# New instruction lists, and new transfer costs in the planner, for a chunk-selecting attention followed by an ELU feed-forward layer

## The chip, the cores and the metric

The kernel runs on one core of a Trainium2 chip. The metric is the device time of one execution in microseconds. It is given as the median of several executions; a profile is taken of one execution, and has a time of its own.

## The reference

Four batches, eight heads, 768 positions, head size 64. Keys stand in 24 chunks of 32. For each query an upper bound of its score with every chunk is computed from the chunk's least and greatest key, and the six best chunks at or before the query's own are kept. Attention runs over the keys of these chunks (and only over earlier positions). The eight heads' results, side by side, go through a layer of 512 to 2048 and back with an ELU between.

```python
k_min, k_max = np.min(k_chunks, axis=3), np.max(k_chunks, axis=3)
ub = np.sum(np.maximum(q[..., None, :] * k_min[:, :, None], q[..., None, :] * k_max[:, :, None]), axis=-1)
ub = np.where(causal, ub, -1e9)
top_chunks = np.argsort(ub, axis=-1)[..., -6:]
scores = scale * np.matmul(q, k.transpose(0, 1, 3, 2))
scores = np.where(sel & (pos[:, None] >= pos[None, :]), scores, -1e9)
attn = softmax(scores)            # written out with max, exp, sum + 1e-9
x = (attn @ v).transpose(0, 2, 1, 3).reshape(3072, 512)
h = x @ w_in
out = np.where(h > 0, h, np.exp(np.minimum(h, 0)) - 1) @ w_out
```

Inputs and output are float32; the products run in bfloat16.

## The kernel before

Heads are handled in pairs (16 pairs, four for each batch), each in two halves of 384 queries. The steps of a pair, with the lines that the profile shows:

- Loads. The four pairs of batch 0 come in halves through staging tiles `gT` (`first_prep`: k and q at L663, v at L668). All later pairs come whole into tiles `f` (`pair_prep`: k and q at L592 in four transfer starts each, 128-byte packets; v at L634 in two starts). SP issues nearly all of them; four q loads of the start are issued by ACT; POOL issues the eight weight transfers (`weights`, L560 and L564).
- Preparation. Batch 0: TensorE transposes (L685), ACT copies out of PSUM (L695, L717, L721), DVE chunk minima and maxima (L704, L711). Later pairs: DVE block transposes (L604, L622) and reductions (L608), ACT L625. POOL casts to bfloat16 (L737, and L728 or L638 for v).
- Selection, for two pairs at once (`quad_sel`): TensorE bounds (L771), DVE transpose, maxima, comparison and transpose back (L787, L799, L804, L810), POOL puts the selection into extra rows of the query tile (L821).
- Attention (`pair_attend`): TensorE scores (L863), ACT exp (L890), POOL causal cut (L909), TensorE values (L922), DVE normalisation (L935, L938), TensorE transpose (L947), ACT copy (L950).
- Feed-forward for half a batch (`mlp`): TensorE up (L972), ACT exp and, in some steps, relu (L982, L987), DVE ELU (L990, L1000, L1005, L1011, L1016), TensorE down (L1032, in four parts for each of three row tiles), ACT copy to one of three `osb` buffers (L1041), SP store (L1046).

The program is straight-line code, and each engine executes its own list in order. The order is not left to a scheduler: every operation gets a number as it is added to a plan, and `QUEUE` holds, for each of the five engines, the numbers in the order in which they are to be emitted. `Plan.order` walks the five lists with a small model of the machine (durations, PSUM and SBUF buffers as numbered slots, the TensorE clock, and the transfers in `served`); from this clock come the order in which the lists are merged into one program and the buffer that each operation gets. The order on each engine is that of the list, whatever the model says. An operation waits, on the chip, for the data that it reads and for the buffer that it takes.

Operations that are spoken of below, by number:

- 13, 31, 47, 65: SP's loads of k, first half, of pairs 0, 1, 2, 3; 163, 181, 197, 215: the second halves; 165, 183, 199, 217: q, second halves; 17, 51, 167, 201: v loads of three starts each. On PE, 19, 35, 53, 69 transpose the first halves of k.
- 331, 333, 335, 337: POOL's transfers of `w_in`; 339 to 345: of `w_out`.
- 415, 421, 427 and 497, 503, 509: ACT's copies of the first six output tiles to `osb`; 416, 422, 428, 498, 504, 510: SP's stores of them.
- 915, 964, 966 (L592, four starts each), 961 (L634, two starts): loads of later pairs.
- 1097 with 1098, and 1091 with 1092: scores on PE (L863) with their exp on ACT (L890).

A list is walked like this, and an operation starts no earlier than its inputs, its buffers and its list allow:

```python
turn = {e: [ops[n] for n in QUEUE[e]] for e in QUEUE}
...
o = turn[e][0]
r = max(t, o.ready)
```

Of the kernel before, what the change touches and what calls it, by code (L numbers as in the profile page):

```python
# [85 lines left out]
    ],  # L86
    "ACT": [
# [20 lines left out]
    ],  # L108
# [5 lines left out]
    ],  # L114
# [43 lines left out]
class Plan:  # L158
# [71 lines left out]
    SHARE = {128: 1.0, 256: 0.35, 512: 0.3, 768: 0.3, 1024: 0.3, 2048: 0.5}  # L230
    HEAVY = 0.088
    RAMP = 240.0
    PAUSE = ((0.0, 2.28), (17.2, 17.8), (21.6, 22.4), (30.5, 31.3))
    LANDED = 0.75

    def served(self, rings, t, until):

        while True:
# [5 lines left out]
            for a, b in self.PAUSE:  # L244
                if a <= t < b:
                    heads = []
# [867 lines left out]
```

## Time and profile before

| | us |
|---|---|
| median of three runs | 273.88 |
| lowest, highest | 272.23, 274.41 |
| the profiled execution | 273.46 |
| its span, first to last instruction | 271.8 |
| TensorE busy in it | 258.6 |
| DVE, ACT, POOL busy | 206.8, 200.0, 118.3 |

The granted TensorE clock was 0.998 of full speed. The profile page gives one execution: busy time of each engine, 40 slices of the span, DMA queues, the chain of work that ended last, the costliest groups of instructions with the idle time before them and what ended it, and DMA issues. Further views of the same trace give busy time by stretch, waits by pair of lines, the chain in order of time, and timelines of an engine. PE is TensorE's products, PEld its weight loads, SPq SyncE's queue.

### The profile page before, as it was taken

The numbers are of one execution on the slowest core, as the hardware profiler recorded it, in microseconds if no ns is written. First come the engines' busy times: TensorE is split into PE (matmuls) and PEld (weight loads), VectorE is DVE, ScalarE is ACT, GpSimd is POOL, SyncE is SP. The second block draws the span as 40 slices with busy tenths as digits, with TensorE's granted clock in tenths as the row PEclk, the third lists the DMA queues.
The fourth block names the chain that finished last, engine by engine and source line by source line (L and its number), as shares of the span: only waits on it lengthen the run. The fifth ranks groups of instructions, "written<-read, shape, count | busy, mean of one in ns | idle before, by whom it ended". The sixth has DMA issues, their size and how long they took to land.

```text
span 271.8 us, 6603 instructions
## 1 busy us (share of the span) xinstructions
PE 258.6 (95%) x2456; PEld 160.0 (59%) x2456; DVE 206.8 (76%) x532; ACT 200.0 (74%) x375; POOL 118.3 (44%) x209
## 2 busy tenths in 40 slices
PE   3898899999999899999999999999999999999995
PEld 3787566655565455655565556665666655555544
DVE  5698979899999979889998867786666875137530
ACT  3899999846996589989899478977898744243512
POOL 3577783155876696870874055544330000000000
PEclk9999999999999999999999999999999999999999
DMA  7997999999999995999931010000210101110113
GB/s 218 266 211 124 205 216 214 164 176 151 148 203 130 192 169 115 139 156 201 240 103 41 1 58 22 0 2 3 76 41 1 41 2 39 39 41 0 65 53 116
DMA packets 112624, 29.79 MB, mean 110 GB/s; under 512 B 101200, under 2 KB 109648, under 8 KB 112592
## 3 DMA queue, kind: packets, MB, share of 16 engines
q1 hardware_dynamic: 107280, 24.39, 48.5%
q0 software_dynamic: 4224, 4.19, 9.3%
q10 hardware_dynamic: 1088, 0.79, 0.9%
q8 instruction: 19, 0.31, 0.5%
q14 instruction: 13, 0.11, 0.1%
HBM read 27.26 MB, written 6.29 MB: 123 GB/s over the span
## 4 chain that ended last, share of the span: by engine, by line
PE 78%; ACT 7%; DVE 6%; DMA 6%; issue 1%; SPq 1%; POOL 0%; DVEq 0%; ACTq 0%; POOLq 0%
PE psH L972 20%; PE psM L1032 20%; PE psS L863 10%; PE psS L972 8%; PE psMT L1032 8%; PE psO L922 6%; ACT pt L890 3%; DMA w_in_sb<-in_moe_w_in_dram 3%; PE psS L771 2%; ACT lhs L695 2%; PE psT L947 2%; DMA out_dram<-osb 1%; PE psMT L685 1%; DMA gT<-in_k_dram 1%; PE psH L685 1%
## 5 line engine op out<-in xcount | busy, mean ns | idle before, releaser
L890 ACT ACTIVATE pt<-psS 128x768 bf16<-128x768 f32 (+1 forms) x120 | 89.8, 781 | 11.3 <-PE psS L863 6.7
L972 PE MATMUL psH<-xT,w_in_sb 128*128 128x384 bf16 x384 | 73.7, 326 | 0.5 <-DMA w_in_sb<-in_moe_w_in_dram 0.4
L1032 PE MATMUL psM<-w_out_sb,gT 128*128 128x512 bf16 x288 | 72.1, 379 | 0.0
L972 PEld LDWEIGHTS <-w_in_sb 128*128 128x128 bf16 x512 | 47.7, 97 | 33.1 <-issue 1.3
L863 PE MATMUL psS<-rhs,lhs 88*128 88x384 bf16 (+4 forms) x304 | 54.6, 283 | 2.8 <-ACT pt L890 2.8
L1032 PEld LDWEIGHTS <-gT 128*128 128x128 bf16 x400 | 37.3, 97 | 33.0 <-DVE gT L1016 0.5
L982 ACT ACTIVATE f<-psH 128x384 f32<-128x384 f32 x96 | 47.0, 506 | 7.0 <-PE psH L972 6.1
L909 POOL TENSOR_SCALAR_AFFINE_SELECT pt<-pt 128x512 bf16<-128x512 bf16 (+1 forms) x48 | 24.7, 522 | 61.6 <-ACT pt L890 58.1
L1011 DVE SCALAR_TENSOR_TENSOR t<-f,psH 128x384 bf16<-128x384 f32 x56 | 30.1, 547 | 12.9 <-ACT f L982 12.4
L863 PEld LDWEIGHTS <-lhs 88*128 88x128 bf16 x304 | 27.4, 98 | 17.8 <-issue 3.0
L737 POOL CAST rhs<-f 64x768 bf16<-64x768 f32 (+1 forms) x40 | 27.7, 698 | 20.4 <-DVE f L622 8.6
L821 POOL COPY rhs<-selt 24x576 bf16<-24x576 bf16 (+2 forms) x40 | 22.7, 566 | 24.2 <-DVE selt L810 22.5
L922 PEld LDWEIGHTS <-pt 128*128 128x128 bf16 x672 | 28.3, 98 | 7.4 <-issue 1.0
L1016 DVE SCALAR_TENSOR_TENSOR gT<-psH,t 128x384 bf16<-128x384 f32 x56 | 30.5, 551 | 1.1
L922 PE MATMUL psO<-vext,pt 128*128 128x65 bf16 x672 | 31.1, 194 | 0.1
L950 ACT ACTIVATE xT<-psT 128x384 bf16<-128x384 bf16 x32 | 15.6, 497 | 11.9 <-PE psT L947 11.9
L972 PE MATMUL psS<-xT,w_in_sb 128*128 128x384 bf16 x128 | 22.9, 326 | 0.0
L982 ACT ACTIVATE f<-psS 128x768 f32<-128x768 f32 x16 | 13.0, 811 | 13.5 <-PE psS L972 13.5
L990 DVE SCALAR_TENSOR_TENSOR gT<-f,psH 128x384 bf16<-128x384 f32 x40 | 21.3, 541 | 2.0 <-ACT psH L987 1.3
L1032 PE MATMUL psMT<-w_out_sb,gT 128*128 128x512 bf16 (+1 forms) x112 | 22.6, 349 | 0.0
L737 POOL CAST lhs<-f 64x768 bf16<-64x768 f32 x24 | 19.7, 823 | 6.4 <-DVE f L604 5.5
L987 ACT ACTIVATE psH<-psH 128x384 f32<-128x384 f32 x40 | 20.2, 512 | 0.0
(55 smaller groups left out, 278.9 us busy)
## 6 DMA issues: line engine op xcount, KB each, us to landing
out_dram<-osb SPq DMA_DIRECT2D x23, 256.0 KB, 2.2
f<-in_k_dram SPq DMA_DIRECT2D x48, 96.0 KB, 3.9
f<-in_q_dram SPq DMA_DIRECT2D x48, 96.0 KB, 3.8
f<-in_v_dram SPq DMA_DIRECT2D x24, 192.0 KB, 3.9
w_in_sb<-in_moe_w_in_dram POOLq DMA_DIRECT2D x4, 512.0 KB, 9.2
w_out_sb<-in_moe_w_out_dram POOLq DMA_DIRECT2D x4, 512.0 KB, 14.7
gT<-in_k_dram SPq DMA_DIRECT2D x8, 192.0 KB, 4.3
gT<-in_v_dram SPq DMA_DIRECT2D x12, 128.0 KB, 4.2
```

Of the source, the lines that this page charges most:

```text
L737: nc.gpsimd.tensor_copy(out=o, in_=i)
L821: eng.tensor_copy(out=dst.rearrange("c h (i two x) -> c h i two x", two=2, x=32)[:, :, :, odd, :], in_=tiles[st][r0:r0 + NCH, c0:c0 + n].r ...
L863: nc.tensor.matmul(p_s[:, hd, pc:pc + w], lhsT=tiles[pt_["kb"]][0:64 + NCH, hd, 128 * kb:128 * kb + 128], rhs=tiles[pt_["qb"]][0:64 + NCH, ...
L890: lambda bs=bs, pt=pt, wtot=wtot, lo=lo, at=at: nc.scalar.activation(out=tiles[pt][:, :, lo:lo + wtot], in_=tiles[bs[0]][:, :, at:at + wto ...
L909: nc.gpsimd.affine_select(out=a, in_=a, compare_op=AOT.is_ge, fill=0.0, base=0, pattern=pat, channel_multiplier=-1)
L922: nc.tensor.matmul(po[:, hd, qi, :], lhsT=tiles[pt][:, hd, off:off + 128], rhs=tiles[pt_["vx"]][:, 6 * hd + kb, :], start=(kb == 0), stop= ...
L972: nc.tensor.matmul(ph, lhsT=w_in_sb[:, kk, f0:f0 + 128], rhs=tiles[XT[4 * b + kk]][:, c0:c0 + HALF], start=(kk == 0), stop=(kk == NKK - 1))
L982: lambda e=e, view=view: nc.scalar.activation(out=halves(e)[:, 0:step], in_=view(), func=AF.Exp),
L990: lambda e=e, view=view, fc=fc, gt=gt: nc.vector.scalar_tensor_tensor(out=tiles[gt][:, fc:fc + step, :], in0=halves(e)[:, 0:step], scalar= ...
L1011: lambda e=e, t=t, view=view: nc.vector.scalar_tensor_tensor(out=tiles[t][:, 0:step], in0=halves(e)[:, 0:step], scalar=1.0, in1=view(), op ...
L1016: lambda t=t, view=view, fc=fc, gt=gt: nc.vector.scalar_tensor_tensor(out=tiles[gt][:, fc:fc + step, :], in0=view(), scalar=0.0, in1=tiles ...
L1032: nc.tensor.matmul(pm, lhsT=tiles[gt][:, fc, 128 * tt:128 * tt + 128], rhs=w_out_sb[:, fc, x0:x1], start=(fc == 0), stop=(fc == NFC - 1))
```

## The change

All five lists are replaced. Each holds the same numbers as before in another order: of PE's 574 places 485 hold another operation, of DVE's 370, 252, of ACT's 378, 285, of POOL's 196, 164, of SP's 77, 53. No operation moves to another engine, and none is added or dropped. The planner's model of transfers changes too: more pauses, the start of a weight transfer as a delay, another share where two queues carry packets of different size, another start delay of ACT's loads, and a later landing of weight parts.

SP's list up to the store of operation 422, before and after (starts are counted from the code: one for each load of batch 0's k and q, three for its v, four for L592, two for L634, one for a store):

```diff
-        13, 163, 31, 47, 17, 65, 165, 217, 183, 51, 181, 197, 201, 215, 199, 511, 167, 513, 528, 530, 545, 525,
-        559, 562, 547, 564, 913, 542, 915, 944, 961, 576, 930, 932, 947, 964, 428, 927, 949, 1317, 498, 978,
-        504, 966, 1315, 1334, 1329, 1349, 1366, 1346, 1332, 422, 1368, 1363, 510, 1351, 416, 818, 1380, 824,
+        13, 31, 65, 47, 17, 51, 163, 183, 165, 197, 181, 167, 215, 199, 201, 217, 511, 513, 528, 530, 545, 559,
+        525, 562, 547, 564, 542, 913, 576, 947, 944, 932, 930, 428, 915, 964, 961, 949, 498, 927, 978, 966,
+        1317, 504, 1315, 422, 1332, 1334, 1349, 1366, 1346, 416, 510, 1368, 1351, 1329, 1380, 818, 1363, 824,
```

The start of PE's list, ACT's around copy 497, POOL's around transfer 331, and PE's and ACT's around 1097 and 1098:

```diff
 PE
-        19, 25, 35, 41, 59, 53, 69, 75, 169, 81, 106, 175, 90, 191, 185, 122, 203, 131, 93, 209, 219, 225, 147,
+        19, 35, 25, 41, 53, 69, 59, 75, 81, 169, 191, 106, 175, 185, 122, 203, 90, 93, 219, 209, 131, 231, 225,
 ACT
-        ... 482, 625, 483, 486, 490, 696, 692, 677, 497, 715, 694,
+        ... 482, 483, 486, 490, 692, 696, 715, 497, 677, 712, 694,
 POOL
-        ... 128, 212, 213, 229, 331, 228, 238, 237, 333, 335, 239, 240, 337, 180, 339, 341, 287, 343, 288,
+        ... 212, 127, 130, 128, 129, 331, 228, 229, 213, 237, 238, 333, 335, 239, 240, 180, 519, 288, 287, 337,
 PE
-        ... 827, 875, 1008, 1064, 828, 1097, 879, 1091, 996, 1000, 999, 998, 997, 1001, 863, 843, 871, 1383,
-        1095, 855, 895, 901, 887, 1081, 1082, 1084, 1083, 1085, 1086, 896, 1113, 891, 902, 1131, 903, 1100,
+        ... 827, 883, 828, 1135, 1091, 863, 871, 843, 1383, 855, 887, 891, 895, 901, 902, 903, 896,
+        996, 998, 999, 1000, 997, 1001, 897, 1097, 1113, 1004, 1064, 904, 1081, 1082, 1084, 1085, 1083, 1086,
 ACT
-        ... 1092, 864, 844, 845, 1098, 872, 865, 873, 856, 1096, 888, 1114, 892, 1377, 905, 1005, 1132,
+        ... 864, 844, 845, 872, 873, 829, 856, 888, 1377, 892, 1092, 1005, 1114, 1098, 1065, 899, 1101,
```

The planner:

```diff
-    ALONE = {128: 0.0138, 256: 0.0188, 512: 0.036, 768: 0.0368, 1024: 0.055, 2048: 0.085}
+    ALONE = {128: 0.0138, 256: 0.0188, 512: 0.036, 768: 0.0376, 1024: 0.055, 2048: 0.085}
...
-    PAUSE = ((0.0, 2.28), (17.2, 17.8), (21.6, 22.4), (30.5, 31.3))
+    PAUSE = ((0.0, 2.28), (17.2, 18.0), (21.8, 22.6), (30.5, 31.3), (53.0, 54.0), (61.0, 62.0), (67.0, 68.2), (80.6, 81.6), (85.4, 86.2), (98.0, 99.0), (108.0, 109.0), (117.0, 118.0))
...
             if heavy and heavy[0][4]:
-                heavy[0][1] += self.RAMP
+                heavy[0][0] = t + self.RAMP * self.HEAVY / 16
                 heavy[0][4] = 0
+                continue
...
+            if not heavy and len(heads) == 2:
+                (e0, h0), (e1, h1) = heads
+                c0, c1 = self.ALONE[h0[2]], self.ALONE[h1[2]]
+                if max(c0, c1) > 1.5 * min(c0, c1):
+                    rate[e0] = 16 / c0 * (0.75 if c0 < c1 else 0.25)
+                    rate[e1] = 16 / c1 * (0.75 if c1 < c0 else 0.25)
...
-        add("DMA", 0.0, -20.0, lambda: None, reads=[("asked", i)], writes=[name], lat=plan.LANDED)
+        add("DMA", 0.0, -20.0, lambda: None, reads=[("asked", i)], writes=[name], lat=plan.LANDED + (0.8 if i else 0.3))
...
-            move=(0 if eng == "SP" else 1, 1.08 if eng == "SP" else 1.3, 0.533, starts, packets, size), **kw)
+            move=(0 if eng == "SP" else 1, 1.08 if eng == "SP" else 1.75, 0.533, starts, packets, size), **kw)
```

The changed file is seven lines longer from `served` on, so L663 before is L670 after, and so on for every line number above.

156 rows, old and new, of the table QUEUE are left out of this document.

## The prediction

> **What bounds the kernel now.** I read the page first, then busy time by stage, then the chain, the waits and the timelines of the places where TensorE stands.
>
> ```profile
> span 271.8 us, 6603 instructions
> ...
> PE 258.6 (95%) x2456; PEld 160.0 (59%) x2456; DVE 206.8 (76%) x532; ACT 200.0 (74%) x375; POOL 118.3 (44%) x209
> ```
>
> The next rows are stretches of the span: length, then busy time of PE, weight load, DVE, ACT and POOL, the granted clock, the DMA share (it counts overlapping packets, so it can pass 1) and GB/s.
>
> ```profile
> 4.20:14.00 9.80, 8.82 (x90) 7.54 (x91) 6.18 (x19) 7.45 (x17) 4.26 (x9) 1.00 1.15 286
> 14.00:35.00 21.00, 18.87 (x315) 15.43 (x313) 19.57 (x84) 20.11 (x46) 15.81 (x32) 1.00 1.11 179
> 35.00:57.00 22.00, 21.51 (x241) 14.40 (x238) 19.36 (x39) 18.80 (x36) 10.01 (x17) 1.00 1.24 195
> 57.00:98.00 41.00, 39.00 (x350) 21.68 (x348) 40.31 (x104) 30.38 (x55) 28.64 (x45) 1.00 1.14 164
> 98.00:210.00 112.00, 112.00 (x1090) 68.00 (x1089) 89.97 (x235) 96.58 (x184) 56.49 (x92) 1.00 0.39 79
> 210.00:258.00 48.00, 48.00 (x322) 26.87 (x320) 26.91 (x43) 22.57 (x36) 0.64 (x1) 1.00 0.08 31
> 258.00:271.80 13.80, 10.44 (x65) 6.06 (x62) 2.56 (x4) 2.77 (x5) 0.00 (x0) 0.96 0.24 88
> ```
>
> Four regimes follow. From 14 to 35 us ACT is the full engine (20.11 of 21). From 57 to 98 DVE is (40.31 of 41), with PE close behind. From 98 to 258 PE never stands: 160 of 160. The last 13.8 us are the final products and their stores. A list that orders the same instructions can win only where PE, or the engine that PE follows, stands: before 98 us. After that it can only lose.
>
> PE's records overlap, so "busy" needs a second reading, the pitch in the chain (start, length, what):
>
> ```profile
> 95.93 1.73 PE psM L1032 x8
> ...
> 115.27 0.65 PE psH L972 x4
> ...
> 119.17 0.86 PE psM L1032 x4
> ```
>
> Four products of L1032 advance the chain by 0.86 us and four of L972 by 0.65, and from 95.93 us on the chain is made almost wholly of such pieces of PE. I take the full PE stretches as truly full.
>
> The Trainium skill (Perfetto Trace Analysis, section Identifying the Most-Contended Engine) holds that matmul busy time does not measure the headroom of TensorE and that the share of weight loads does. By that rule 59% would leave 111 us of room on PE, and a new order could win much more than I allow. The pitch in the chain does not agree: the room is in the waits alone.
>
> **The change, part by part.** No instruction is added, removed or resized; durations stay. The cost constants steer only the planner's clock, which merges the fixed lists and picks buffers, so they issue nothing: 0 us. What acts are the places in the five lists.
>
> (1) *The store that holds ACT at 93 us* (88 to 95 us).
>
> ```profile
> 84.84 4.94 SPq L592 DMA_DIRECT2D f<-in_k_dram  x8
> 89.82 0.61 SPq L1046 DMA_DIRECT2D out_dram<-osb  x1
> ...
> 89.82 3.55 DMA out_dram<-osb
> ...
> 90.84 0.81 ACT L890 ACTIVATE pt<-psS 128x768 bf16<-128x768 f32 x1 [0.17 <-PE psS L863]
> 93.39 0.60 ACT L1041 ACTIVATE osb<-psM 128x512 f32<-128x512 f32 x1 [1.74 <-DMA out_dram<-osb]
> ...
> 94.74 0.49 PE L863 MATMUL psS<-rhs,lhs 88*128 88x384 bf16 x2 [1.36 <-ACT pt L890]
> 95.44 0.48 PE L863 MATMUL psS<-rhs,lhs 88*128 88x384 bf16 x2 [0.22 <-ACT pt L890]
> ```
>
> Two of the three `osb` buffers hold outputs whose stores (416, 422) stand far down SP's list, so one buffer rotates. Its store, 428, issues at 89.82 behind loads and lands 3.55 us later; ACT's next copy (497) waits 1.74 us for it, the exps behind the copy wait too, and PE stands 1.36 + 0.22 = 1.58 us. In the new SP list 428 stands ahead of 915, 964 and 961: 4 + 4 + 2 = 10 starts fewer. Eight starts take 4.94 us, so ten take 6.2: issue near 83.6, landing near 87.2. ACT reaches the copy at 90.84 + 0.81 = 91.65 (on ACT's list 497 only trades places with one exp), so 4.5 us to spare, and the wait goes. How much of 1.58 stays won? DVE is next to be late:
>
> ```profile
> 91.00:98.00 7.00, 5.42 (x38) 2.81 (x36) 6.64 (x10) 4.76 (x8) 4.78 (x9) 1.00 1.35 189
> ```
>
> DVE stands only 7 - 6.64 = 0.36 us here. If DVE binds, 0.36 is all; if its next results are early enough, 1.58. DVE's order puts loads' transposes between PE's needs and has slack from 98 on (89.97 of 112), so I take the middle: -1.0 (bounds -1.58 to -0.36).
>
> (2) *The first loads* (0 to 14 us).
>
> ```profile
> 0.81 1.97 SPq L663 DMA_DIRECT2D gT<-in_k_dram  x4
> ...
> 6.04 0.51 SPq L663 DMA_DIRECT2D gT<-in_k_dram  x1
> ...
> 12.22 1.57 SPq L668 DMA_DIRECT2D gT<-in_v_dram  x3
> ...
> 14.71 0.51 SPq L663 DMA_DIRECT2D gT<-in_q_dram  x1
> ...
> 7.04 0.49 ACT L717 ACTIVATE f<-psMT 128x384 f32<-128x384 f32 x1 [0.80 <-PE psMT L685]
> ...
> 12.01 0.48 ACT L695 ACTIVATE lhs<-psH 64x384 bf16<-64x384 f32 x1 [0.49 <-PE psH L685]
> ...
> 11.13 0.85 PE L685 MATMUL psH<-ident_f,gT 128*128 128x128 f32 x6 [0.87 <-ACT qa L721]
> ...
> gT<-in_k_dram SPq DMA_DIRECT2D x8, 192.0 KB, 4.3
> ```
>
> The old list sends a second-half k (163) as SP's second load and the fourth pair's first-half k (65) as its eighth, at 6.04; the transposes of that one start at 11.13, 5.1 us later. The new list sends 13, 31, 65, 47: 65 issues near 1.8 with the first group. The ACT waits at 7.04 and 12.01, 0.80 + 0.49 = 1.29 us, are what this can win, since ACT is full right after. Against it: the last k/q load (217) now stands one v load (three starts, 1.57 us by the row) behind the place where the last one was, so near 16.3, and a load takes 4.3 us. What comes in earlier at first comes in later at the end. Bounds: -1.29, and +1.57 if the late load goes wholly through to ACT. The transposes that need 217 stand some 5 us after its issue, 0.7 more than a load takes, so I stay nearer the gain: -0.5.
>
> The Trainium skill (DMA: Bandwidth & Descriptors, section Issuing engines are not separate DMA queues) states that transfers of all issuing engines share the same 16 DMA engines and interleave. The stage's DMA share of 1.15 agrees that they are full; by that rule reordering moves lateness about, this term is 0, and the sum would be 0.5 us higher.
>
> (3) *The weights* (24 to 36 us).
>
> ```profile
> PEld L972 <- DMA w_in_sb<-in_moe_w_in_dram: 0.5, 1, 0.5
> ...
> 23.33 1.52 POOL L737 CAST rhs<-f 64x384 bf16<-64x384 f32 x3 [0.97 <-ACT f L717]
> 24.79 0.92 POOL L560 DMA_DIRECT2D w_in_sb<-in_moe_w_in_dram  x1
> ```
>
> The first weight transfer (331) stood behind three casts and now stands behind one of them: two casts fewer, 1.52 / 3 = 0.51 each, 1.0 us earlier. PE's one wait for weights is 0.5. I take -0.3 (0 to -0.5). The later w_out parts move back on POOL, behind transfers that are still queued: 0.
>
> (4) *SP's own wait*.
>
> ```profile
> 99.55 1.06 SPq L634 DMA_DIRECT2D f<-in_v_dram  x2
> 104.48 0.36 SPq L1046 DMA_DIRECT2D out_dram<-osb  x1
> ```
>
> Store 504 held SP from 100.61 to 104.48; now load 966 goes first. Behind it are loads for POOL and DVE; PE does not stand there (112 of 112), so 0.
>
> (5) *Everything else*: nearly every operation changes place by a few positions. In the full PE stretch this cannot win; a result that comes one step late costs. I take +0.3; the bounds are 0 and the fourth rival's 3.5.
>
> **Sum**: -1.0 - 0.5 - 0.3 + 0.3 = -1.5 us. The profiled execution took 273.46 us (271.8 span, 1.66 around it); it would become 271.96. The median of the runs before is 273.88, 0.42 above it, so the forecast is 273.88 - 1.5 = 272.4 us; its own range is 271.0 to 273.6.
>
> **The rivals.**
> *All waits go* (B): 1.58 + 1.29 + 0.5 = 3.4, nothing lost after 98 us: 270.5. For it: each wait has a visible cause that the lists move the right way. Against: ACT and DVE are full behind them, so a shift must pass through both.
> *The new lists do not help* (C): the store's wait goes and DVE (40.31 of 41) takes its place; the early loads even out: 273.9.
> *Slower* (D): an exp that ACT reaches before its scores, at 147 us.
>
> ```profile
> 143.30 0.49 PE L863 MATMUL psS<-rhs,lhs 88*128 88x384 bf16 x2
> ...
> 147.27 0.80 ACT L890 ACTIVATE pt<-psS 128x768 bf16<-128x768 f32 x1
> ...
> 147.00:154.00 7.00, 7.00 (x75) 3.75 (x75) 6.07 (x14) 4.61 (x10) 0.62 (x2) 1.00 0.01 4
> 154.00:161.00 7.00, 7.00 (x55) 3.92 (x54) 5.67 (x25) 4.04 (x9) 2.66 (x4) 1.00 0.10 37
> ```
>
> Scores 1097 move behind seven L972 groups (0.65 each in the chain), six L1032 groups (0.86) and some small ones, about 11 us; their exp 1098 moves back only some nine ACT operations of about 0.5, 4.4 us. Its lead was 147.27 - 143.79 = 3.5, so ACT would stand 11 - 4.4 - 3.5, about 3 to 3.5 us, with its list blocked. If a product group's exp (L982) is needed meanwhile, PE stops as long: 272.4 + 3.5 = 275.9, and up to 278 if the neighbour (1091, 1092) does the same. Against it: ACT has 2.39 + 2.96 = 5.35 us free in these 14 us, and in the new list the L982 exps of this stage all stand ahead of 1098. It decides only if ACT's wait outlasts that cover.
>
> **How the numbers follow.** Forecast 0.48, B 0.15, C 0.12, D 0.25. About 1%, 2.7 us, is what a measurement of this kernel can tell from no change: under 271.1 is faster, over 276.6 slower. Faster: B 0.15 and the low end of the forecast 0.08, 0.23. Slower: a little over half of D, 0.14. Within 1%: 0.63. The range 270.4 to 276.6 leaves out about half of B and the top of D.
>
> **What would show it.** Right: ACT's copy at about 91 us without a DMA wait and store 428 issued before 85; the fourth first-half transpose of k starting before 11; weights issued near 23.5 and no PE wait on them; PE still full from 98 to 258. Wrong: DVE over 6.9 of 7 from 91 to 98 with PE waiting on it (C); ACT waiting over 3 us for L863 near 150 with PE short of full there (D); new PE waits on k or q loads between 15 and 25 us.

## The result, and the profile after

| | before | after |
|---|---|---|
| median of five runs, us | 273.68 | 271.17 |
| lowest, highest | 272.23, 274.41 | 270.49, 271.98 |
| the profiled execution, its span | 273.46, 271.8 | 271.23, 269.5 |

The new lists are faster: ratio 0.9913 [0.9887, 0.9939], 2.5 us. In a second set of runs the same kernel gave 0.9948 [0.9917, 0.9979], about 1.4 us. The ratios, here and below, are estimated from single runs of the fast state and are not the quotients of the medians beside them, from which they differ by up to 0.003.

The head of the page, then the stretches of the span as in the prediction (length, then PE, weight load, DVE, ACT, POOL, granted clock, DMA share, GB/s), all of the kernel after:

```profile
span 269.5 us, 6606 instructions
...
PE 257.1 (95%) x2431; PEld 159.9 (59%) x2456; DVE 206.2 (77%) x532; ACT 199.8 (74%) x375; POOL 118.7 (44%) x209
```

```profile
4.20:14.00 9.80, 9.02 (x92) 7.76 (x93) 8.76 (x28) 7.77 (x18) 3.63 (x8) 1.00 1.19 285
14.00:35.00 21.00, 18.64 (x301) 14.77 (x298) 18.25 (x78) 19.85 (x46) 15.88 (x32) 1.00 1.06 177
35.00:57.00 22.00, 21.78 (x247) 14.97 (x250) 19.63 (x39) 19.57 (x37) 11.36 (x18) 1.00 1.23 193
57.00:98.00 41.00, 40.41 (x377) 23.18 (x380) 40.62 (x106) 32.39 (x57) 29.69 (x46) 1.00 1.09 169
98.00:210.00 112.00, 111.35 (x1060) 67.67 (x1069) 88.71 (x237) 96.13 (x185) 55.03 (x90) 1.00 0.40 81
210.00:258.00 48.00, 47.70 (x311) 26.43 (x316) 27.39 (x42) 20.43 (x33) 0.64 (x1) 1.00 0.09 34
```

PE gains 1.4 us of work between 57 and 98 us. Behind 98 us it seems 0.95 us short of full, but the trace lacks 25 of its 2456 products (x2431), so the busy time is not the place to read a loss.

**A ledger from three rows.** ACT's copies of the output tiles are the same work in both kernels. Three of them, operation 415, operation 497 and the last one, cut the span in four. First their rows before (that of 497, at 93.39, stands in the prediction), then after, in ACT's timeline (start, length, and in brackets the idle time ahead of it and who ended it):

```profile
60.69 0.60 ACT L1041 ACTIVATE osb<-psM 128x512 f32<-128x512 f32 x1 [1.61 <-PE psM L1032]
...
268.53 0.38 ACT L1041 ACTIVATE osb<-psMT 128x256 f32<-128x256 f32 x1 [0.97 <-PE psMT L1032]
```

```profile
60.25 0.60 ACT L1048 ACTIVATE osb<-psM 128x512 f32<-128x512 f32 x1 [1.61 <-PE psM L1039]
...
91.00 0.59 ACT L1048 ACTIVATE osb<-psM 128x512 f32<-128x512 f32 x1
...
266.29 0.38 ACT L1048 ACTIVATE osb<-psMT 128x256 f32<-128x256 f32 x1 [1.36 <-PE psMT L1039]
```

| us | to 415 | 415 to 497 | 497 to last copy | last copy to end |
|---|---|---|---|---|
| before | 60.69 | 32.70 | 175.14 | 3.27 |
| after | 60.25 | 30.75 | 175.29 | 3.21 |
| difference | -0.44 | -1.95 | +0.15 | -0.06 |

The sum is -2.30, the difference of the spans. Most of it lies between 415 and 497, where the wait of 1.74 us for a store is gone from the row of 497. The store now issues here, in SP's timeline:

```profile
83.75 0.48 SPq L1053 DMA_DIRECT2D out_dram<-osb  x1
```

### The profile page after: what moved, and what is told of

Read it like the earlier page. It is cut to its first block, busy times and chain, and to the rows that moved or that the text cites. A ratio compares the mean times of both kernels' runs of the same rounds, so it can differ in the third digit from the quotient of the medians.

```text
span 269.5 us, 6606 instructions
## 1 busy us (share of the span) xinstructions
PE 257.1 (95%) x2431; PEld 159.9 (59%) x2456; DVE 206.2 (77%) x532; ACT 199.8 (74%) x375; POOL 118.7 (44%) x209
## 4 chain that ended last, share of the span: by engine, by line
PE 82%; DVE 7%; DMA 4%; ACT 3%; issue 2%; POOL 1%; DVEq 0%; POOLq 0%; ACTq 0%
PE psH L979 22%; PE psM L1039 20%; PE psS L870 10%; PE psS L979 8%; PE psMT L1039 8%; PE psO L929 6%; DMA w_in_sb<-in_moe_w_in_dram 3%; PE psS L778 3%; PE psT L954 2%; PE psH L692 1%; ACT lhs L702 1%; DMA gT<-in_k_dram 1%; DVE f L611 1%; DVE f L629 1%; DVE kx L615 1%
## 5 line engine op out<-in xcount | busy, mean ns | idle before, releaser
L897 ACT ACTIVATE pt<-psS 128x768 bf16<-128x768 f32 (+2 forms) x120 | 89.4, 780 | 13.6 <-PE psS L870 6.8
L979 PE MATMUL psH<-xT,w_in_sb 128*128 128x384 bf16 x384 | 74.7, 326 | 0.7 <-DMA w_in_sb<-in_moe_w_in_dram 0.5
L1039 PE MATMUL psM<-w_out_sb,gT 128*128 128x512 bf16 x266 | 68.5, 379 | 1.2
L870 PE MATMUL psS<-rhs,lhs 88*128 88x384 bf16 (+4 forms) x304 | 53.7, 283 | 0.2
L929 PEld LDWEIGHTS <-pt 128*128 128x128 bf16 x672 | 26.9, 98 | 5.8 <-issue 0.3
L929 PE MATMUL psO<-vext,pt 128*128 128x65 bf16 x672 | 29.1, 193 | 0.1
```

The lines of the kernel that those rows point to most:

```text
L870: nc.tensor.matmul(p_s[:, hd, pc:pc + w], lhsT=tiles[pt_["kb"]][0:64 + NCH, hd, 128 * kb:128 * kb + 128], rhs=tiles[pt_["qb"]][0:64 + NCH, ...
L897: lambda bs=bs, pt=pt, wtot=wtot, lo=lo, at=at: nc.scalar.activation(out=tiles[pt][:, :, lo:lo + wtot], in_=tiles[bs[0]][:, :, at:at + wto ...
L929: nc.tensor.matmul(po[:, hd, qi, :], lhsT=tiles[pt][:, hd, off:off + 128], rhs=tiles[pt_["vx"]][:, 6 * hd + kb, :], start=(kb == 0), stop= ...
L979: nc.tensor.matmul(ph, lhsT=w_in_sb[:, kk, f0:f0 + 128], rhs=tiles[XT[4 * b + kk]][:, c0:c0 + HALF], start=(kk == 0), stop=(kk == NKK - 1))
L1039: nc.tensor.matmul(pm, lhsT=tiles[gt][:, fc, 128 * tt:128 * tt + 128], rhs=w_out_sb[:, fc, x0:x1], start=(fc == 0), stop=(fc == NFC - 1))
```

## The experiments

The theory after the result: the store 428 alone carries most of the gain; it was under-priced; the early terms carry little. The rivals: the new middle part wins by its whole order, not by the store; or the early loads win and the store is chance. Every run stands beside runs of the kernel before on its own chip; ratios are to those.

**Only the store, and thirds of the new lists.** The first takes the lists of before and moves one number on SP:

```diff
-    576, 930, 932, 947, 964, 428, 927,
+    576, 930, 428, 932, 947, 964, 927,
```

> The lists of before; on SP's list alone the store 428 stands ahead of 932 instead of behind 964 (932, 947, 964: twelve load starts fewer ahead of it). Theory 1 (the wait of ACT's copy for this store is the main gain): the copy no longer waits, 1.2 to 1.8 us faster than before, 0.994 to 0.996. Rival 2 (DVE binds there, and it is the new lists of DVE, PE and ACT between 57 and 105 us that win): ACT's wait goes but DVE takes its place, 0 to 0.4 us.

The next three take the new order on all five engines in one part of the span and the old one in the others; all three carry the planner of after. The cuts are where both orders have emitted the same set of operations: about 57 and 105 us.

```diff
 QUEUE, each engine: old | old | old
+mid:                old | new | old
+first57:            new | old | old
+late:               old | old | new
```

> The lists of before up to about 57 us and from about 105 us on, the new lists between. Theory 1: the store's wait is in this part, 1.5 to 2.0 us faster than before (0.993 to 0.995). Rival 2: about the same, 1.8 us, and more than the run with the store alone by over 1 us. Rival 3 (the gain is spread over all stages): 0.8 us.

> The new lists up to about 57 us, the lists of before from there. Theory 1: the first loads and the weights come out even or win little, 0.2 to 0.6 us faster than before (0.998 to 0.999). Rival 3 (spread): 0.8 us. With the store's wait still in, the gain may also be swallowed at 93 us: then 0.

> The lists of before up to about 105 us, the new lists after it. Theory 1: PE is full there in both, so 0.0 us, within 0.2. Rival 3: 0.5 to 0.8 us faster. The forecast's own term for small losses there: 0.3 us slower.

| | median, us | before, us | ratio |
|---|---|---|---|
| store | 272.08 | 273.02 | 0.9949 [0.9927, 0.9972] |
| mid | 271.66 | 273.02 | 0.9944 [0.9921, 0.9967] |
| first57 | 273.63 | 273.02 | 0.9994 [0.9964, 1.0024] |
| late | 273.54 | 273.02 | 1.0005 [0.9979, 1.0032] |

The one moved store, and the middle part that holds it, gain 0.5% each; the other two parts gain nothing that can be measured. `late` carries the planner's new costs, and `store` the old ones, so the gain does not come from the planner. Copies 415, 497 and last in `store`:

```profile
60.96 0.60 ACT L1037 ACTIVATE osb<-psM 128x512 f32<-128x512 f32 x1 [1.61 <-PE psM L1028]
...
91.82 0.59 ACT L1037 ACTIVATE osb<-psM 128x512 f32<-128x512 f32 x1
...
266.96 0.38 ACT L1037 ACTIVATE osb<-psMT 128x256 f32<-128x256 f32 x1 [0.98 <-PE psMT L1028]
```

From 415 to 497 it takes 30.86, against 32.70 before and 30.75 with all new lists: of the 1.95 us of that stretch the single store carries 1.84 in these profiles. Behind 497 `store` takes 175.14, to the hundredth what before takes: nothing of the gain is given back. Copies 415 and 497 in `mid`, 30.75 apart, then all three in `late`:

```profile
60.78 0.60 ACT L1044 ACTIVATE osb<-psM 128x512 f32<-128x512 f32 x1 [1.61 <-PE psM L1035]
...
91.53 0.59 ACT L1044 ACTIVATE osb<-psM 128x512 f32<-128x512 f32 x1
```

```profile
60.73 0.60 ACT L1044 ACTIVATE osb<-psM 128x512 f32<-128x512 f32 x1 [1.61 <-PE psM L1035]
...
93.27 0.60 ACT L1044 ACTIVATE osb<-psM 128x512 f32<-128x512 f32 x1 [1.56 <-DMA out_dram<-osb]
...
269.05 0.38 ACT L1044 ACTIVATE osb<-psMT 128x256 f32<-128x256 f32 x1 [1.36 <-PE psMT L1035]
```

`late` keeps the wait (32.54), and takes 175.78 behind 497, 0.64 more than before.

`first57` asks where early gains go. Copies 415 and 497 in its profile, and in the chain the flight of the store that 497 waits for:

```profile
59.38 0.60 ACT L1044 ACTIVATE osb<-psM 128x512 f32<-128x512 f32 x1 [1.61 <-PE psM L1035]
...
91.27 0.60 ACT L1044 ACTIVATE osb<-psM 128x512 f32<-128x512 f32 x1 [0.32 <-DMA out_dram<-osb]
```

```profile
88.74 2.50 DMA out_dram<-osb
```

It comes to 415 1.31 us earlier than before does. With the store in its old place SP issues it at 88.74, at the end of an unbroken row of loads, as before does at 89.82. In this profile the store thus came 1.08 us earlier too and flew 2.50 us instead of 3.55, and the early gain was kept: this execution (271.33) was the fastest of twelve with a median of 273.63. That in the other executions a later issue or a usual flight eats the early gain is argued; the next run has a profile of such a case.

**The store alone put back, and the kernel after once more.** In the new lists:

```diff
-    930, 428, 915, 964, 961, 949,
+    930, 915, 964, 961, 428, 949,
```

> The changed kernel with the store 428 alone put back behind 915, 964 and 961 on SP's list (ten load starts). Theory 1 (ACT's wait for this store is the main term): the wait of about 1.5 us comes back and most of the gain goes, 1.2 to 1.8 us slower than the changed kernel, 0.995 to 0.998 of before. Rival 2 (DVE binds, the store does not matter in the new lists): as fast as the changed kernel, within 0.4 us.

> The changed kernel once more, on the chip of the next three, to compare with them: 0.990 to 0.994 of before.

The lists of after with the store put back took 275.43 us beside 273.45 of before, 1.0054 [1.002, 1.0088]; after again took 272.29, 0.9948 [0.9917, 0.9979]. One number in one list is thus worth about 3 us here (3.1 by the medians, 2.9 by the ratios), and without it the new lists are slower than the old; expected was that they would stay a little faster. Copies 415 and 497 of the kernel with the store put back, and the flight in its chain:

```profile
59.61 0.60 ACT L1044 ACTIVATE osb<-psM 128x512 f32<-128x512 f32 x1 [1.61 <-PE psM L1035]
...
93.05 0.60 ACT L1044 ACTIVATE osb<-psM 128x512 f32<-128x512 f32 x1 [2.56 <-DMA out_dram<-osb]
```

```profile
89.21 3.81 DMA out_dram<-osb
```

At 415 it is 1.08 us ahead of before; at 497 it is 0.34 ahead. ACT waits 2.56 instead of 1.74: what came early waits longer for a store that SP issues behind its loads (at 89.21) and that flies 3.81. The early terms and the store's term are one chain, not two terms to be added. From 415 to 497 it takes 33.44, 2.69 more than after, which is most of the 3 us. (Behind 497 it takes 175.99, 0.70 more than after; this, and the 1.45 us from the 273.98 of the profiled execution to its median, are not explained.)

The profile of after's second run took 273.06 against 271.23 of the first. Its three copies:

```profile
60.96 0.60 ACT L1048 ACTIVATE osb<-psM 128x512 f32<-128x512 f32 x1 [1.61 <-PE psM L1039]
...
91.73 0.59 ACT L1048 ACTIVATE osb<-psM 128x512 f32<-128x512 f32 x1
...
268.15 0.38 ACT L1048 ACTIVATE osb<-psMT 128x256 f32<-128x256 f32 x1 [1.36 <-PE psMT L1039]
```

The ledger gives 60.96, 30.77 and 176.42: +0.71 ahead of 415 and +1.13 behind 497. Two waits are new, one in PE's timeline and one in ACT's:

```profile
52.82 1.02 PE L1039 MATMUL psM<-w_out_sb,gT 128*128 128x512 bf16 x4 [0.81 <-DMA w_out_sb<-in_moe_w_out_dram]
```

```profile
109.83 0.60 ACT L1048 ACTIVATE osb<-psM 128x512 f32<-128x512 f32 x1 [1.19 <-DMA out_dram<-osb]
```

```profile
107.48 0.47 SPq L1053 DMA_DIRECT2D out_dram<-osb  x1
```

The first is for the `w_out` parts that moved back on POOL. The second is copy 509 waiting for store 504, which now stands behind load 966 and in this execution issued at 107.48, against this in the first profile:

```profile
103.72 0.60 SPq L1053 DMA_DIRECT2D out_dram<-osb  x1
```

**More work for DVE.** To see whether DVE took the place of the store's wait, two of its transposes of a load (951 and 968, 0.95 us each) are done twice, which changes no value; in the lists of before and in those of after:

```diff
             o.emit()
+            if o.n in (951, 968):
+                o.emit()
```

> The kernel before with the same two transposes (at 92.8 and 95.0 us) done twice. DVE stood 0.36 us there and 2.0 us in waits for PE behind 98 us, so if that slack is what let the store's gain through: 0 to 0.6 us slower than before (1.000 to 1.002), clearly less than in the changed kernel. If DVE binds before as well: 1.2 to 1.9 us slower (1.004 to 1.007).

> The changed kernel with DVE's block transposes 951 and 968 (at 90.6 and 95.4 us, 0.95 us each) done twice: 1.9 us more of DVE at the place where the store's wait was. If DVE is what PE now follows from 57 to about 112 us (the forecast's reason for taking 1.0 of 1.58): 1.2 to 1.9 us slower than the changed kernel. If DVE had slack and took nothing back: under 0.5 us slower.

On before: 273.94 beside 273.45, 1.0023 [0.9998, 1.0048]. On after: 273.09, 0.9992 [0.997, 1.0015], 0.8 above after's 272.29. By these times alone the two costs, 0.5 and 0.8, cannot be told apart. In the ledger they can. Copy 497, the next one (503) and the last one in before, then in after, with the two transposes doubled:

```profile
92.84 0.60 ACT L1041 ACTIVATE osb<-psM 128x512 f32<-128x512 f32 x1 [1.41 <-DMA out_dram<-osb]
...
103.79 0.62 ACT L1041 ACTIVATE osb<-psM 128x512 f32<-128x512 f32 x1
...
268.48 0.38 ACT L1041 ACTIVATE osb<-psMT 128x256 f32<-128x256 f32 x1 [0.97 <-PE psMT L1032]
```

```profile
90.93 0.59 ACT L1048 ACTIVATE osb<-psM 128x512 f32<-128x512 f32 x1
...
101.92 0.59 ACT L1048 ACTIVATE osb<-psM 128x512 f32<-128x512 f32 x1
...
268.19 0.38 ACT L1048 ACTIVATE osb<-psMT 128x256 f32<-128x256 f32 x1 [1.36 <-PE psMT L1039]
```

From the one to the other the 1.9 us of DVE work cost 0.50 in before (175.64 against 175.14) and 1.97 in after (177.26 against 175.29). Nearly all of it is there by copy 503, which comes 10.95 behind 497 in before with the doubled work (10.45 without it, copy 503 at 103.84), and 10.99 in after (9.22 without it in both of after's profiles, at 100.22 and 100.95). The timed 0.8 is less than 1.97, and less than the 1.2 to 1.9 expected. The second profile of after suggests why: it lost 1.13 us to the wait for store 504, which the late copy 509 of the doubled kernel does not have, and against its 176.42 the doubled kernel takes 0.84 more. PE's timeline of after with the two transposes:

```profile
100.69 0.81 PE L954 MATMUL psT<-ident_b,on 128*128 128x128 bf16 x6 [1.23 <-DVE on L945]
```

The windows say why. DVE from 98 to 105 us, in before and then in `store` (third busy time):

```profile
98.00:105.00 7.00, 7.00 (x91) 4.13 (x90) 5.59 (x12) 6.62 (x13) 6.56 (x11) 1.00 0.67 124
```

```profile
98.00:105.00 7.00, 6.94 (x84) 3.81 (x84) 6.93 (x29) 6.61 (x14) 6.14 (x11) 1.00 0.80 186
```

And what DVE waited for between 84 and 104 us in before (total, times, longest); `store` has no such row:

```profile
DVE rc L935 <- PE psO L922: 1.6, 1, 1.6
```

Before, DVE had 1.41 us of idle right behind the store's wait, because PE was late for it. With the wait gone that idle is used up, and DVE is the next bound. The 0.50 fits: it is about the 1.9 us of added work less the 1.41 of idle.

**The two late waits, and the other stores.** Store 504 alone is put back ahead of load 966 in the lists of after:

```diff
-    978, 966, 1317, 504, 1315,
+    978, 504, 966, 1317, 1315,
```

> The changed kernel with the store 504 alone moved on SP's list ahead of 966 and 1317, as it stood before. If the wait of copy 509 for this store (1.2 us in the second profile of the changed kernel, none in the first) is what makes the changed kernel's times spread: the slow half of its times goes, 0.3 to 0.9 us faster in the median, 0.989 to 0.992 of before. If the spread comes from the loads of the first 60 us alone: as the changed kernel, 0.991 to 0.995, same spread.

It took 270.70 us beside 273.26, 0.9901 [0.9867, 0.9935], the best median of all; its interval overlaps that of after, so better than after is not shown. Six of its ten runs lie between 270.29 and 270.75, four between 271.60 and 272.63. Its profile is one of the four (271.61): no wait at 509 any more, 175.29 behind 497, but the one for `w_out` is there:

```profile
52.48 1.02 PE L1035 MATMUL psM<-w_out_sb,gT 128*128 128x512 bf16 x4 [1.17 <-DMA w_out_sb<-in_moe_w_out_dram]
```

The other two `osb` buffers are held by stores 416 and 422, far down SP's list. Moved ahead, in after (416 before 542, 422 before 947) and in before (416 before 913, 422 before 944, and 428 as in `store`):

```diff
 osb_three
-    564, 542, 913, 576, 947, ... 1315, 422, 1332, ... 1346, 416, 510
+    564, 416, 542, 913, 576, 422, 947, ... 1315, 1332, ... 1346, 510
 before_three
-    564, 913, 542, 915, 944, ... 1332, 422, 1368, ... 1351, 416, 818
+    564, 416, 913, 542, 915, 422, 944, ... 1332, 1368, ... 1351, 818
```

> The changed kernel with the stores 416 and 422 moved up on SP's list (ahead of 542 and 947), so that all three osb buffers turn and no copy waits for the store just before it. If stores are the whole of the matter: 0.5 to 1.2 us faster than the changed kernel, 0.988 to 0.991 of before, and narrower times. If the two stores delay loads that something waits for (each start takes about 0.5 us): 0 to 1 us slower than the changed kernel.

> The lists of before; on SP's list alone the stores 416, 422 and 428 moved up (ahead of 913, 944 and 932). If the new lists' gain is the stores: as fast as the changed kernel or faster, 0.990 to 0.994 of before. If the new lists win 0.5 us or more elsewhere: 0.995, as with store 428 alone, and slower than the changed kernel with the same stores moved by 0.5 us or more.

In after's lists: 271.10 beside 273.26, 0.9913 [0.9885, 0.9942]. In before's: 272.36, 0.9966 [0.9943, 0.9989]. With three buffers in turn no copy waits for a store in the profile of `before_three`; in that of `osb_three` one does, 0.45 us at 236.43, as in after (0.43 at 237.16). After's lists are still 1.3 us better than before's. In the two profiles copy 415 is 1.68 us apart (61.20 and 59.52), and from there to the end they differ by less than 0.1. Last, `osb_three` with two early DVE operations (7 and 10) moved behind 40, to see whether they hold the first reductions of k:

```diff
 DVE
-    6, 0, 8, 9, 12, 11, 22, 23, 7, 10, 38, 24, 39, 40, 56,
+    6, 0, 8, 9, 12, 11, 22, 23, 38, 24, 39, 40, 7, 10, 56,
```

> The changed kernel with stores 416 and 422 moved up, and on DVE's list the bf16 copy of the identity (7) and one row copy (10) moved behind the first k reductions (behind 40). In the changed kernel these two hold the reductions of the second k by 1.3 us and PE waits 0.6 us at 10.7 us. If the first loads then set the pace anyway (the first 1.3 us won were given back by 18 us): the same as with the stores alone, within 0.3 us. If ACT's wait of 0.8 us at 12.2 us is worth something: 0.3 to 0.8 us faster than with the stores alone.

271.68, 0.9925 [0.9896, 0.9954]: no gain over `osb_three`.

**The start, over all profiles.** Six kernels have the old lists up to 57 us and seven the new ones (without the last). PE's first product with `w_in` starts at 32.76 on average in the old (32.59 to 33.06) and at 32.04 in the new (31.78 to 32.47). Copy 415 starts at 60.81 (60.47 to 61.20) and 60.05 (59.38 to 60.96). So the new start is 0.7 to 0.8 us ahead, with more spread; the two late ones of the seven, 60.96 and 60.63, are the two with the `w_out` wait (the eighth new start, `osb_three_rows`, has 0.27 us of it). Where the store stands in its old place, this gain can be lost at it, as in `store_back`.

## Why the prediction was right, and where its steps failed

The forecast of 272.4 was on the right side, and the result, 271.17, is 1.2 us under it, close to the lower edge of its own range (271.0). It stays just within the 1% that the prediction took for the limit of a measurement (271.1), though both intervals exclude no change. The second set, about 1.4 us under before, is nearly the -1.5 of the sum, so that the sum as a whole was too small is not shown.

Step (1), the store: right in kind; by the ledger the term was too small, by the times it may have been right. -1.0 was taken between -0.36 and -1.58. The ledger of `store` shows -1.84, and all eight profiles with the store moved (the doubled transposes left out) take 30.75 to 30.86 from 415 to 497, against 32.70 and 32.54 of the old lists in before and `late`. The medians of `store` and before differ by 0.94, and the ratio 0.9949 is 1.4 us, with an interval from 0.8 to 2.0. Copy 497 starts at 91.00 without a wait (91.65 forecast) and the store issues at 83.75 (83.6 forecast). The argument that DVE has only 0.36 us free failed: the window was cut at 98 us, and right behind it DVE stood another 1.41, waiting for PE's late products of the values (`psO`). An engine that waits for the stalled one is not a bound on what the stall is worth. By the ledger the upper bound was too low as well: 1.84 is more than PE's idle of 1.58 and nearer to ACT's wait of 1.74.

Step (2), the first loads: the size was right (-0.5 forecast, about -0.7 at 32 us by the profiles), the place in the sum wrong. The fourth pair's transposes (operation 69, the second half of the first row below) moved ahead of 11 us as forecast, but ACT and PE soon wait again:

```profile
8.58 1.50 PE L692 MATMUL psH<-ident_f,gT 128*128 128x128 f32 x12 [0.19 <-ACT f L724]
...
11.33 0.88 PE L692 MATMUL psMT<-ident_f,gT 128*128 128x128 f32 x6 [0.59 <-DVE kx L711]
...
22.12 0.88 PE L692 MATMUL psMT<-ident_f,gT 128*128 128x128 f32 x6 [0.19 <-DMA gT<-in_q_dram]
```

```profile
12.24 0.87 ACT L724 ACTIVATE f<-psMT 128x384 f32<-128x384 f32 x2 [0.78 <-PE psMT L692]
```

Taken alone the gain is 0 in time (`first57`, 0.9994), which fits a store that eats it in most executions; a new wait on q of the kind that was feared is 0.19 us at 22.12. By what the prediction drew from the Trainium skill (DMA: Bandwidth & Descriptors, section Issuing engines are not separate DMA queues) the term would have been 0. The time of `first57` agrees with that; the profiles do not, with the new start 0.7 us ahead at 32 us.

Step (3), the weights: failed. The first and the last weight transfer in POOL's timeline, the last one in that of before, and PE's wait in after:

```profile
23.33 0.92 POOL L567 DMA_DIRECT2D w_in_sb<-in_moe_w_in_dram  x1
...
43.40 0.75 POOL L571 DMA_DIRECT2D w_out_sb<-in_moe_w_out_dram  x1
```

```profile
36.85 0.75 POOL L564 DMA_DIRECT2D w_out_sb<-in_moe_w_out_dram  x1
```

```profile
35.10 0.82 PE L979 MATMUL psH<-xT,w_in_sb 128*128 128x384 bf16 x4 [0.47 <-DMA w_in_sb<-in_moe_w_in_dram]
```

The first transfer issues when it was to (23.5 forecast), but PE's 0.5 for `w_in` stays. And the 0 for the later `w_out` parts failed: the last one issues 6.55 us later, and two of the seven profiles show PE waiting 0.81 and 1.17 us for `w_out`.

Step (4), store 504 behind load 966: 0 in the first profile, 1.13 us in the second. "PE does not stand there" was read from one execution; the cover was thin, not absent.

Step (5), everything else: +0.3 forecast, +0.15 behind 497 in after.

The rivals. B (270.5) asked for all waits to go; they did not, and the time still came near it since the store was worth more. C saw the right successor: DVE is full from 91 to 98 in after, as C's sign asked, but PE does not wait for it there, and it costs nothing until work is added:

```profile
91.00:98.00 7.00, 6.89 (x62) 4.16 (x62) 7.00 (x11) 6.67 (x11) 6.56 (x11) 1.00 1.13 202
```

A wait like D's came, for another reason, and cost nothing:

```profile
151.74 0.81 ACT L897 ACTIVATE pt<-psS 128x768 bf16<-128x768 f32 x1 [3.84 <-PE psO L929]
...
147.00:154.00 7.00, 6.95 (x49) 3.62 (x49) 6.27 (x31) 2.23 (x5) 0.00 (x0) 1.00 0.11 38
```

By the place in ACT's list this is the exp 1092, the neighbour, and not 1098, which follows at 154.82 without such a wait. It stands 3.84 us (forecast 3 to 3.5), behind products of the values rather than scores; before had 2.20 of the same kind at 152.09. That the size came near the forecast is luck. PE goes on at 6.95 of 7: its cover outlasted the wait.

Open: how much of the 1.3 us between `before_three` and `osb_three` is the start. Their two profiles put all of it ahead of copy 415, but the start's average over all profiles is 0.7 to 0.8; the rest is inside the intervals. Open too: why the new lists with the store put back are slower than before. That the two groups of times of `s504_first` are those with and without the `w_out` wait is likely (271.61 less what the wait costs is its lower group) but one profile shows it.

## What to carry to other kernels

Look for a transfer whose issue time is set by a queue of other transfers and not by the engines' progress: it is a clock for what waits for it, and what is won ahead of it can be lost there (0.74 of 1.08 us in `store_back`). Price the removal of a stall by what the next engine does when it is fed on time, in a window that reaches past the stall; an engine that idles because of the stall is no bound. Cut the span at a few operations that both kernels have: three rows of one line showed in which stretch the gain lies, where busy time could not.

## What was not expected of the hardware

One list does not give one execution. With the same instructions, after's two profiles differ by 1.83 us, and two waits for transfers account for it (0.81 for `w_out`, 1.19 for a store) that one execution has and the other has not. The flight of one and the same store, 256 KB behind loads, took 2.50, 3.55 and 3.81 us in the profiles of `first57`, before and `store_back`, and ACT's wait for it was 0.32, 1.74 and 2.56. From this spread of 1.31 us, an estimate: beside a busy DMA a cover of less than about 1.5 us should be counted as a chance, not as 0.
